# Second layer's input scale from a bound taken when x is written, and late keys turned two ranks later

## The chip, the cores and the metric

One program runs on one core of a Trainium2 chip. The metric is the device time of one execution in microseconds (us), lower is better. The kernel before takes 1208.0 us, the median of three runs (1207.2 to 1209.08).

## The reference

Attention with 32 kept keys per row, followed by two feed-forward layers on the same tokens. Batch 4, 8 heads, 576 tokens, head width 64; the 2304 rows of attention output have 512 columns.

```python
scores = q @ k.T / 8;  kth = 32nd largest of each row
attn = softmax(where(scores >= kth, scores, -1e9))
x = (attn @ v) laid out as (2304, 512)
x = (sigmoid(x @ w_gate) * (x @ w_val)) @ w_out     # 512 -> 1536 -> 512
h = x @ w_in;  out = (relu(h) ** 2) @ w_out2        # 512 -> 2048 -> 512
```

## The kernel before

**Tiles and chunks.** The 2304 rows are 18 tiles of 128. `CHUNKS` groups them: chunks 0 to 5 hold one tile, chunks 6 to 11 hold two (6 and 7, then 8 and 9, up to 16 and 17). A chunk passes through attention, then through both feed-forward layers (`moe32` for chunks 0 and 1 in float32, `moe` for chunks 2 to 11). `attention` runs over units: one head of one tile. Scores of a unit come from four matmuls (`scores`, L395) into S, then VectorE finds the 32 largest in seven rank steps, MAX8 and MATCH_REPLACE8 in turn (`rank`, L406 and L407). ScalarE and GpSimd make the weights, a transposing DMA turns them (PT, L480), and `values16` (L531) multiplies by v and writes x (tile `xs`) for chunks 6 to 11.

**Two float16 halves.** In chunks 2 to 11 each operand of a feed-forward matmul is a pair of float16 tiles, high and low, whose sum stands for the scaled float32 value; a product is three matmuls. So an input needs a power-of-two scale before it can be cut in two. For attention output of chunks 6 to 11 that scale comes from v (`xfac`, `ix`), for chunks 2 to 5 from a sum of squares (`split_x`).

**The second layer's input.** Layer 1 ends in two PSUM tiles, `accs` (L828). `moe` then makes `x2` from them (L854 to L870): ScalarE squares each half (L858), TensorE sums the squares over the partitions with a matrix of ones into `x2pq` (L860, a buffer of the pool `ps_w`), VectorE takes the maximum (L863) and three small steps make the scale `sy` and its inverse `iy` (`pow2_scale`, L140 to L146). Only then ScalarE writes the high half (L867) and VectorE the low half (L868), and the second layer's first matmuls `ph` (L893) can start. In chunks 3 to 10 the program has matmuls of the next chunk's first layer to put in between (`nxt`, `NPRE` = 2 column blocks, `pg` and `pv` at L788); the last chunk, 11, has none.

**Keys.** `prep_keys` loads one head pair's keys of one batch (tiles kn and ke, L161 and L163), transposes them on TensorE into `kpt` (L174), copies the rounded part out on ScalarE (kp, L181), subtracts it on VectorE (L182), and stores both to DRAM (`ks`, four DMAs at L188). Units load them from there (`kst`, L345). Each of the 4 batches has 4 head pairs, so there are 16 such turns. Those of batch 2 are made while chunk 6 is in attention (kpt between 381 and 473 us), those of batch 3 during chunk 8 (600 to 687 us), each at the start of a head pair (`head`), about one chunk ahead of their use.

**Order of the work.** Every engine and every DMA queue runs its instructions in a fixed order. It is made when the program is built: a scheduler that simulates a time line picks, engine by engine, by priorities set around the code (`tc.high_priority`, `at`). All DMAs named here are issued by SyncE (SP), one after another; an issue that waits holds all behind it. The list `later` holds steps put off to a given rank step: `(k, function, arguments)` is run just after rank step k of the unit at hand, and a dependency without a semaphore (`NOSYNC`) tells the scheduler to place the step behind that rank instruction. The kernel uses it for v (`KB`, `KC`). It looked at the first entry of the list alone.

The lines that decide where the second layer may start:

```python
nc.scalar.activation(sq[:, h * KH : (h + 1) * KH], srcs[h], AF.Square)          # L858
nc.tensor.matmul(pq[:, 0:N], ones, sq[:, c], ...)                               # L860
nc.vector.reduce_max(cm, pq[:, 0:N], axis=AX.X)                                 # L863
sy, iy = pow2_scale(cm, small)                                                  # L864
nc.scalar.activation(x2[:, 0, hs], srcs[h], AF.Copy, scale=sy)                  # L867
```

Of the kernel before, what the change touches and what calls it, by code (L numbers as in the profile page):

```python
# [9 lines left out]
BF16 = mybir.dt.bfloat16  # L10
F32 = mybir.dt.float32
F32R = mybir.dt.float32r
I32 = mybir.dt.int32
U32 = mybir.dt.uint32
AF = mybir.ActivationFunctionType
ALU = mybir.AluOpType
# [5 lines left out]
P = 128  # L22
# [48 lines left out]
GLATE = 30.0  # L71
EARLY = ("wg", "wv")
PB = 10
KB = 4
KC = 6
FIRST = 2
# [8 lines left out]
def tile_topk_attention__then__two_moe_layers(  # L85
# [47 lines left out]
    ones = one.to_broadcast([P, P])  # L133


    def pow2_scale(norm, t, squared=True, s=None):

        n = t[:, 0:1]
        shift, e = (24, 62) if squared else (23, 126)
        nc.vector.tensor_scalar(n, norm.bitcast(I32), shift, None, op0=ALU.logical_shift_right)  # L140
        if s is None:
            s = t[:, 1:3]
        nc.vector.tensor_scalar(
            s[:, 0:1], n, -float(2**23), float((127 + e + TB) * 2**23), op0=ALU.mult, op1=ALU.add
        )
        nc.vector.tensor_scalar(  # L146
            s[:, 1:2], n, float(2**23), float((127 - e - TB) * 2**23), op0=ALU.mult, op1=ALU.add
        )
        f = s.bitcast(F32)
        return f[:, 0:1], f[:, 1:2]  # L150
# [5 lines left out]
    def prep_keys(b, hp, keep=False):  # L156

        src = k[b, 2 * hp : 2 * hp + 2]
        kn = apool.tile([P, S], F32, tag="S", bufs=SB, name=f"kn_{b}_{hp}")
        kv = kn[:, 0 : CB * P].rearrange("p (c h d) -> p c h d", c=CB, h=2)  # L160
        nc.sync.dma_start(kv, src[:, 0:SM].rearrange("j (p c) d -> p c j d", c=CB))  # L161
        ke = apool.tile([ST, 2, D], F32, tag="qn", bufs=2, name=f"ke_{b}_{hp}")
        nc.sync.dma_start(ke, src[:, SM:S].rearrange("h p d -> p h d"))  # L163
        kh = apool.tile([P, S], F32R, tag="kst", bufs=KST, name=f"kp_{b}_{hp}")
        kl = kn.bitcast(F32R)
        if keep:
            kl = mpool.tile([P, S], F32R, tag="m4", bufs=M4, name=f"kl_{b}_{hp}")
            kloc[(b, hp)] = (kh, kl)
        for lo, hi in ((0, CB), (CB, NB)):
            pt = ps_t.tile([P, 512], F32, tag="tr", name=f"kpt_{b}_{hp}_{lo}")  # L170
            w = 0
            for c in range(lo, hi):
                kp = P if c < CB else ST
                nc.tensor.transpose(  # L174
                    pt[:, w : w + kp],
                    (kv[:, c] if c < CB else ke).rearrange("p h d -> p (h d)"),
                    ident[0:kp, 0:kp],
                )
                w += kp
            c0 = lo * P  # L180
            nc.scalar.copy(kh[:, c0 : c0 + w], pt[:, 0:w])  # L181
            nc.vector.tensor_tensor(  # L182
                kl[:, c0 : c0 + w], pt[:, 0:w], kh[:, c0 : c0 + w], op=ALU.subtract
            )
        d = dpool.tile([2, 2, D, S], F32R, name=f"ks_{b}_{hp}", tag=f"ks_{b}_{hp}")
        for a, t in enumerate((kh.bitcast(F32), kl.bitcast(F32))):
            for j in range(2):
                nc.sync.dma_start(d.bitcast(F32)[j, a], t[j * D : (j + 1) * D])  # L188
        for j in range(2):
            kscr[(b, 2 * hp + j)] = d[j].rearrange("a d s -> (a d) s")  # L190
# [565 lines left out]
        return xs, ix  # L756


    ahead = {}

    def start(ci):
# [47 lines left out]
    def moe(ci, nxt=None):  # L809
# [42 lines left out]
        KH = KM // 2  # L852
        srcs = [a[:, 0 : KH * N].rearrange("p (d n) -> p d n", d=KH) for a in accs]
        with tc.high_priority(offset=XUP):  # L854
            sq = x2[:, 1].bitcast(BF16)
            pq = ps_w.tile([P, 512], F32, tag="wk", name=f"x2pq_{ci}")
            for h in range(2):
                nc.scalar.activation(sq[:, h * KH : (h + 1) * KH], srcs[h], AF.Square)  # L858
                for c in range(h * KH, (h + 1) * KH):
                    nc.tensor.matmul(pq[:, 0:N], ones, sq[:, c], start=(c == 0), stop=(c == KM - 1))  # L860
            small = mpool.tile([P, 8], I32, tag="sc", bufs=3, name=f"x2s_{ci}")
            cm = small.bitcast(F32)[:, 3:4]
            nc.vector.reduce_max(cm, pq[:, 0:N], axis=AX.X)  # L863
            sy, iy = pow2_scale(cm, small)  # L864
            for h in range(2):
                hs = slice(h * KH, (h + 1) * KH)
                nc.scalar.activation(x2[:, 0, hs], srcs[h], AF.Copy, scale=sy)  # L867
                nc.vector.scalar_tensor_tensor(  # L868
                    x2[:, 1, hs], srcs[h], sy, x2[:, 0, hs], op0=ALU.mult, op1=ALU.subtract
                )  # L870
# [2 lines left out]
                nxt()  # L873
        usc, i2 = layer2_scales()

        us = small.bitcast(F32)[:, 4:6]
        nc.vector.scalar_tensor_tensor(us[:, 0:1], ix, iy, usc, op0=ALU.mult, op1=ALU.mult)
        nc.vector.scalar_tensor_tensor(
# [181 lines left out]
    def attention():  # L1060
# [62 lines left out]
        def tail(n, after=None):  # L1123
# [30 lines left out]
            if j == 1 and i == len(pr.tts) - 1:  # L1154
                if pr.ci < TCI:
                    pr.values()
                    xdone[pr.ci] = pr.hp + 1
                if pr.hp == NHP - 1:
                    if pr.ci in PLAIN:
                        xsp[pr.ci] = pr.xt  # L1160
                    elif pr.ci < TCI:
                        xsp[pr.ci] = split_x(pr.ci, pr.xt)
                    else:
                        xsp[pr.ci] = pr.xt, xfacs[pr.ci][0]

        def orders(n):
            a = [(n - 1, k) for k in range(KA, 7)]
# [29 lines left out]
        for n in range(last + 1):  # L1197
            ci = units[min(n, last - 1)][0].ci
            if ci < TCI:
                with tc.high_priority(offset=int(up[0])):  # L1200
                    head(n + 1)
                    tails((False,))
            if n < last:
                pr, pi, j, i = units[n]
                state[n] = pr.softmax_head(j, i, ready.pop(n))
            for u, k in orders(n):
                if u in state:
                    ins = units[u][0].rank(state[u], k)
                    if k == 0 and prev3 is not None:
                        tc.add_manual_dep(  # L1210
                            ins, prev3.name, NOSYNC, reason="two row blocks at a time"
                        )
                    if k == min(KA, 6):
                        prev3 = ins
                    if k == 6:
                        ends[u] = len(seq)
                    seq.append(ins)
                    while later and later[0][0] == k:
                        _, fn, args = later.pop(0)
                        fn(*args, ins)  # L1220
            turns()
            if ci >= TCI:
                head(n + 1)
                tails((False,))
            tails((True,))
            if n > 0:
                pr, pi, j, i = units[n - 1]
                work[n - 1] = pr.softmax(j, i, state.pop(n - 1))
            turns()
            yield  # L1230
# [166 lines left out]
```

## Time and profile before

| | |
|---|---|
| median of 3 runs | 1208.0 us (1207.2 to 1209.08) |
| profiled execution, its own time | 1210.65 us |
| its span, first to last instruction | 1208.5 us |
| mean granted TensorE clock | 0.987 of 2.4 GHz |
| TensorE matmuls busy | 1154.8 us, 96% |
| VectorE busy | 919.9 us, 76% |
| GpSimd busy | 833.8 us, 69% |
| ScalarE busy | 802.8 us, 66% |

An engine's share is an average over a span with three parts: loading and weight preparation up to about 100 us, attention and feed-forward side by side up to about 1040 us, and feed-forward alone until the end. PE is TensorE's matmuls, DVE VectorE, ACT ScalarE, POOL GpSimd, SP SyncE. A group row of the profile gives busy time, mean duration and the idle time of the engine just before; a row of the timeline gives start, duration, engine, line, what is written and read, the count, and in brackets an idle time before it with what ended it.

### The profile page before, as it was taken

The page shows a single profiled execution, that of the slowest core. Times are in us where ns is not written, and L with a number is a line of the kernel's source. Part 1 is how long each engine was busy: PE and PEld are TensorE (multiplying, and loading weights), DVE is VectorE, ACT ScalarE, POOL GpSimd, SP SyncE. Part 2 cuts the span into 40 slices and gives each one's busy share as a digit, 9 for nine tenths or more (in the row PEclk, how much of TensorE's full clock was granted, in tenths as well). Part 3 has the DMA queues.
Part 4 walks back from the last instruction along what each step waited for, and adds up shares of the span by engine and source line. Part 5 has one row for each costly group of instructions (what it writes and reads, how often), then busy time and mean ns, then how long its engine had stood idle before and what let it go on. Part 6 is the DMA issues. An engine that isn't in the chain of part 4 may idle for free. (4 is left out here: it accounts for less than half of the span.)

```text
span 1208.5 us, 30486 instructions
## 1 busy us (share of the span) xinstructions
PE 1154.8 (96%) x11473; PEld 940.1 (78%) x11473; DVE 919.9 (76%) x1921; ACT 802.8 (66%) x1695; POOL 833.8 (69%) x1294
## 2 busy tenths in 40 slices
PE   7879999999899998999999999999999999999998
PEld 5669878977778877787887688768877886886875
DVE  5999788999998878999998799989899878010010
ACT  5999975877876777777678777676677566222122
POOL 1788964788874786978778877987697669324133
PEclk9889999999999999999999999999999999999999
DMA  8998854324544466656675675665455422100000
GB/s 228 367 347 282 300 153 114 82 86 123 160 118 113 97 147 149 150 128 127 123 173 132 138 157 120 130 149 118 73 106 125 88 49 56 38 1 1 18 1 18
DMA packets 241394, 153.64 MB, mean 127 GB/s; under 512 B 191328, under 2 KB 207712, under 8 KB 241248
## 3 DMA queue, kind: packets, MB, share of 16 engines
q1 hardware_dynamic: 241248, 151.70, 49.5%
q8 instruction: 90, 1.47, 0.5%
q14 instruction: 56, 0.46, 0.1%
HBM read 105.25 MB, written 18.09 MB: 102 GB/s over the span
## 5 line engine op out<-in xcount | busy, mean ns | idle before, releaser
L406 DVE MAX8 mx<-W 128x8 f32<-128x576 f32 x432 | 327.8, 759 | 10.8
L407 DVE MATCH_REPLACE8 W<-mx,W 128x576 f32<-128x576 f32 x288 | 213.9, 743 | 0.0
L893 PE MATMUL ph<-x,wi_w 128*128 128x256 f16 (+1 forms) x1920 | 191.9, 254 | 2.5 <-ACT x L867 1.6
L914 PE MATMUL acc<-w_w,rh 128*128 128x512 f16 x768 | 182.1, 379 | 0.8 <-POOL rh L906 0.8
L893 PEld LDWEIGHTS <-wi_w 128*128 128x128 f16 x1920 | 157.0, 99 | 28.7 <-issue 2.9
L478 POOL TENSOR_TENSOR pp<-S,pp 128x512 f16<-128x512 f32 x192 | 137.1, 736 | 1.7
L395 PE MATMUL sp<-kst,qt 128*128 128x288 f32 x608 | 131.7, 327 | 6.8 <-DMA kst<-ks 4.1
L828 PEld LDWEIGHTS <-wo_w 128*128 128x128 f16 x1440 | 118.0, 98 | 18.0 <-issue 5.0
L788 PEld LDWEIGHTS <-wg_w 128*128 128x128 f16 x1440 | 116.9, 98 | 16.9 <-issue 1.7
L788 PEld LDWEIGHTS <-wv_w 128*128 128x128 f16 x1440 | 117.8, 98 | 15.6 <-issue 3.0
L800 DVE TENSOR_TENSOR th<-pv,th 128x512 f32<-128x512 f32 (+1 forms) x60 | 34.6, 577 | 124.6 <-PE pv L788 118.2
L432 ACT ACTIVATE S<-S,mx 128x576 f32<-128x576 f32 x144 | 111.8, 776 | 26.3 <-DVE mx L406 25.5
L914 PEld LDWEIGHTS <-rh 128*128 128x128 f16 x768 | 72.3, 98 | 72.4 <-POOL rh L906 1.0
L406 DVE MAX8 mx<-S 128x8 f32<-128x576 f32 x144 | 107.2, 745 | 14.6 <-ACT S L398 14.4
L398 ACT COPY S<-sp 128x576 f32<-128x576 f32 x144 | 91.7, 637 | 37.6 <-PE sp L395 33.3
L407 DVE MATCH_REPLACE8 W<-mx,S 128x576 f32<-128x576 f32 x144 | 107.0, 743 | 0.0
L788 PE MATMUL pg<-xs,wg_w 128*128 128x256 f16 x864 | 106.2, 273 | 0.4 <-DVE th L800 0.4
L476 POOL TENSOR_SCALAR S<-S,bs 128x576 f32<-128x576 f32 x96 | 71.9, 749 | 50.0 <-ACT pp L475 43.6
L905 POOL TENSOR_TENSOR r<-r 128x512 f32<-128x512 f32 (+1 forms) x80 | 69.7, 871 | 52.8 <-ACT rh L904 51.5
L788 PE MATMUL pv<-xs,wv_w 128*128 128x256 f16 x864 | 103.7, 273 | 0.5 <-DVE x2s L863 0.5
L828 PE MATMUL acc<-gh,wo_w 128*128 128x256 f16 (+1 forms) x1056 | 102.2, 248 | 1.6 <-POOL gh L804 1.6
L475 ACT ACTIVATE pp<-S,bs 128x576 f16<-128x576 f32 x96 | 74.4, 775 | 42.5 <-issue 21.6
(238 smaller groups left out, 2321.4 us busy)
## 6 DMA issues: line engine op xcount, KB each, us to landing
kst<-ks SPq DMA_DIRECT2D x112, 288.0 KB, 3.2
v<-vd SPq DMA_DIRECT2D x32, 320.0 KB, 3.3
wi_r<-in_moe_w_in_dram SPq DMA_DIRECT2D x16, 512.0 KB, 6.2
w_r<-in_moe_w_out_dram SPq DMA_DIRECT2D x16, 512.0 KB, 4.9
qn<-in_q_dram SPq DMA_DIRECT2D x124, 64.0 KB, 2.6
v<-in_v_dram SPq DMA_DIRECT2D x28, 256.0 KB, 3.1
wg_r<-in_moe_w_gate_dram SPq DMA_DIRECT2D x12, 512.0 KB, 6.1
wv_r<-in_moe_w_val_dram SPq DMA_DIRECT2D x12, 512.0 KB, 7.3
```

What stands on the lines that cost most here:

```text
L395: nc.tensor.matmul(sp[:, e, 0:HALF], l, r, start=(x == 0), stop=(x == len(ops) - 1))
L398: nc.scalar.copy(ss.rearrange("p (e s) -> p e s", e=2), sp[:, :, 0:HALF])
L406: return nc.vector.max(m8, st.cur).ins
L407: ins = nc.vector.match_replace(st.wk, m8, st.cur, NEG).ins
L432: nc.scalar.activation(wk, wk, AF.Prelu, bias=kth, scale=-1.0, alpha=1.0 / BIG)
L475: nc.scalar.activation(pp[:, 0:S], wk, AF.Copy, scale=rz)
L476: nc.gpsimd.tensor_scalar(wk, wk, rz, 1.0, op0=ALU.mult, op1=ALU.mult)
L478: nc.gpsimd.tensor_tensor(pp[:, o : o + e - f], wk[:, f:e], pp[:, f:e], op=ALU.subtract)
L788: nc.tensor.matmul(pp[:, e * N : (e + 1) * N], wblk(wd, a, c, f0, P), xs[:, b_, c, :], start=(e == 0 and n == 0), stop=(n == 3 * KM - 1), ...
L828: nc.tensor.matmul(accs[d // 2][:, (d % 2) * N : (d % 2 + 1) * N], wblk("wo", a, f, d * P, P), gh[:, b_, e * N : (e + 1) * N], start=(f == ...
L893: nc.tensor.matmul(ph[:, e * N : (e + 1) * N], wblk("wi", a, c, f0, P), x2[:, b_, c, :], start=(e == 0 and n == 0), stop=(n == 3 * KM - 1) ...
L914: nc.tensor.matmul(acc2[i][:, 0:DM], gh[:, b_, e * N + i * P : e * N + (i + 1) * P], wblk("w2", a, f, 0, DM), start=(f == 0 and x == 0), s ...
```

## The change

There are three parts. First, `x2` of a chunk no longer waits for its own squares. For chunks 6 to 11 `x_squares` squares the high half of x on ScalarE once x is written (behind rank step `KX` = 1 of a following unit), into the single buffer `vo` that the values' halves use too; `x_norm` sums it with four matmuls into a buffer of `ps_t` (behind rank step `KP` = 5), and makes `sy` and `iy` there, lowered by 2^17 (`X2B`), a bound in which the weights' norms stand. For chunks 2 to 5, whose x was scaled by its own norm already, the scale is the constant 2^-17. Second, the keys of batches 2 and 3 are loaded where they were, but turned behind rank step `KK` = 2 of a following unit (`turn_keys`). Third, the list `later` now runs every entry of the rank step at hand, not the first alone.

```diff
+X2B = 17
+KX = 1
+KP = 5
+KK = 2
+KL = (2, 3)
...
         nc.sync.dma_start(ke, src[:, SM:S].rearrange("h p d -> p h d"))
+        if b in KL:
+            later.append((KK, turn_keys, (b, hp, keep, kn, kv, ke)))
+        else:
+            turn_keys(b, hp, keep, kn, kv, ke, None)
+
+    def turn_keys(b, hp, keep, kn, kv, ke, after):
         kh = apool.tile([P, S], F32R, tag="kst", bufs=KST, name=f"kp_{b}_{hp}")
...
+    def x_squares(ci, xt, after=None):
+        N = len(chunks[ci]) * P
+        sq = apool.tile([P, KM, N], BF16, tag="vo", bufs=1, name=f"xq_{ci}")
+        ins = nc.scalar.activation(sq, xt[:, 0], AF.Square)
+        if after is None:
+            x_norm(ci, sq, N)
+        else:
+            tc.add_manual_dep(ins.ins, after.name, NOSYNC, reason="written by then")
+            later.append((KP, x_norm, (ci, sq, N)))
+
+    def x_norm(ci, sq, N, after=None):
+        pq = ps_t.tile([P, 512], F32, tag="tr", name=f"xn_{ci}")
+        for c in range(KM):
+            mm = nc.tensor.matmul(pq[:, 0:N], ones, sq[:, c], start=(c == 0), stop=(c == KM - 1))
+            if after is not None:
+                tc.add_manual_dep(mm.ins, after.name, NOSYNC, reason="squared by then")
+                after = None
+        t = xsmall[ci]
+        cm = t.bitcast(F32)[:, 3:4]
+        nc.vector.reduce_max(cm, pq[:, 0:N], axis=AX.X)
+        x2s[ci] = pow2_scale(cm, t[:, 5:6], s=t[:, 6:8], lower=X2B)
...
         with tc.high_priority(offset=XUP):
-            sq = x2[:, 1].bitcast(BF16)
-            pq = ps_w.tile([P, 512], F32, tag="wk", name=f"x2pq_{ci}")
-            for h in range(2):
-                nc.scalar.activation(sq[:, h * KH : (h + 1) * KH], srcs[h], AF.Square)
-                for c in range(h * KH, (h + 1) * KH):
-                    nc.tensor.matmul(pq[:, 0:N], ones, sq[:, c], start=(c == 0), stop=(c == KM - 1))
-            small = mpool.tile([P, 8], I32, tag="sc", bufs=3, name=f"x2s_{ci}")
-            cm = small.bitcast(F32)[:, 3:4]
-            nc.vector.reduce_max(cm, pq[:, 0:N], axis=AX.X)
-            sy, iy = pow2_scale(cm, small)
+            sy, iy = x2s.pop(ci, (float(2.0**-X2B), float(2.0**X2B)))
             for h in range(2):
                 hs = slice(h * KH, (h + 1) * KH)
                 nc.scalar.activation(x2[:, 0, hs], srcs[h], AF.Copy, scale=sy)
...
                         xsp[pr.ci] = pr.xt, xfacs[pr.ci][0]
+                        if after is None:
+                            x_squares(pr.ci, pr.xt)
+                        else:
+                            later.append((KX, x_squares, (pr.ci, pr.xt)))
...
-                    while later and later[0][0] == k:
-                        _, fn, args = later.pop(0)
-                        fn(*args, ins)
+                    for x in [x for x in later if x[0] == k]:
+                        later.remove(x)
+                        x[1](*x[2], ins)
```

The lines of the changed kernel stand further down, so L867 is L907 there, L174 is L195, L188 is L212 and L345 is L369.

**ScalarE, last chunk.** The first place is the end of chunk 11's first layer on ScalarE (`gh` is the last block of layer 1, `x_11` is x2 of chunk 11, `r` and `rh` belong to layer 2). Before:

```order
L798 ACTIVATE th_5_17985<-pg_5_17935,ix_15515 128x512
L803 CAST gh_5_17989<-th_5_17985 128x512
L858 ACTIVATE x_11_18064<-acc_11_0_17747 128x512
L858 ACTIVATE x_11_18064<-acc_11_1_17748 128x512
L867 ACTIVATE x_11_18064<-acc_11_0_17747,x2s_18072 128x512
L867 ACTIVATE x_11_18064<-acc_11_1_17748,x2s_18072 128x512
L902 ACTIVATE r_0_18110<-ph_0_18085 128x512
```

Now:

```order
L847 ACTIVATE th_5_17952<-pg_5_17902,ix_15482 128x512
L852 CAST gh_5_17956<-th_5_17952 128x512
L907 ACTIVATE x_11_18031<-acc_11_0_17714,ix_15482 128x512
L907 ACTIVATE x_11_18031<-acc_11_1_17715,ix_15482 128x512
L943 ACTIVATE r_0_18066<-ph_0_18041 128x512
```

The two squares are gone, and the two copies that write x2 follow the last block directly; their scale is in the chunk's `ix` tile, which is written some 40 ScalarE instructions earlier.

**TensorE, a turn of late keys.** The second place is the turn of batch 2's last head pair on TensorE (`sp` are scores, `kpt` the turned keys, `ph` layer 2 of chunk 4, `xp` the product with v). Before:

```order
L788 MATMUL pv_5_1_7107<-xt_5_4951,wv_w1_2432 128x128
L395 MATMUL sp_6_6_7615<-kst_6_6_1_7260,qt_6_3_1_7468 128x288 x3
L174 MATMUL kpt_2_3_0_7586<-ident_81,kn_2_3_7581 128x128 x4
L893 LDWEIGHTS wi_w0_2896
L893 MATMUL ph_4_0_7165<-x2_4_7089,wi_w0_2896 128x128
```

Now:

```order
L555 MATMUL xp_6_2_7571<-PT_6_4_7340,v_6_2_1_6169 64x128
L195 MATMUL kpt_2_3_0_7681<-ident_81,kn_2_3_7548 128x128
L555 LDWEIGHTS v_6_2_1_6169
L555 MATMUL xp_6_2_7571<-PT_6_5_7450,v_6_2_1_6169 64x128
L195 MATMUL kpt_2_3_0_7681<-ident_81,kn_2_3_7548 128x128 x3
L934 LDWEIGHTS wi_w4_3139
```

The transposes stood right behind the scores of head pair 3's first unit (`sp_6_6`) and ahead of `ph_4_0`; now they stand inside a product with v, and `ph_4_0` to `ph_4_3` of layer 2 are ahead of them.

**SyncE, the stores of late keys.** The third place is SP's queue at the first turn of batch 3 (`ks` are the four stores, `kst` the loads of keys for a unit's scores, `PT` the transposing DMAs). Before:

```order
L161 DMA kn_3_0_9708<-in_k_dram 128x8x64
L163 DMA ke_3_0_9710<-in_k_dram 64x2x64
L316 DMA qn_10_1_9729<-in_q_dram 128x2x64
L480 DMA_TRANSPOSE PT_8_7_9601<-pp_8_7_9596 128x9x128
L316 DMA qn_10_1_9729<-in_q_dram 128x2x64
L188 DMA ks_3_0_9724<-kp_3_0_9712 64x576 x2
L188 DMA ks_3_0_9724<-kn_3_0_9708 64x576 x2
L316 DMA qn_11_1_9732<-in_q_dram 128x2x64 x2
L345 DMA kst_8_1_2_9737<-ks_2_0_5421 128x576
L345 DMA kst_8_2_2_9906<-ks_2_1_6197 128x576
```

Now:

```order
L176 DMA kn_3_0_9675<-in_k_dram 128x8x64
L178 DMA ke_3_0_9677<-in_k_dram 64x2x64
L504 DMA_TRANSPOSE PT_8_7_9568<-pp_8_7_9563 128x9x128
L340 DMA qn_10_1_9679<-in_q_dram 128x2x64 x2
L350 DMA v_8_0_2_9325<-vd_2_0_5483 128x1280
L504 DMA_TRANSPOSE PT_9_6_9740<-pp_9_6_9735 128x9x128
L230 DMA ve_3_1_10367<-in_v_dram 64x2x64 x2
L340 DMA qn_11_1_9682<-in_q_dram 128x2x64 x2
L212 DMA ks_3_0_9840<-kp_3_0_9828 64x576 x2
L212 DMA ks_3_0_9840<-kn_3_0_9675 64x576 x2
L369 DMA kst_8_2_2_9873<-ks_2_1_6318 128x576
```

The four stores moved behind the load of v and one transposing DMA, and of the two key loads that stood behind them one (`kst_8_1`) now stands earlier in the queue.

## Rows read from the trace of the kernel before

**Rows 1.** The page's busy times: engine, us busy, share, instructions.

```profile
PE 1154.8 (96%) x11473; PEld 940.1 (78%) x11473; DVE 919.9 (76%) x1921; ACT 802.8 (66%) x1695; POOL 833.8 (69%) x1294
```

**Rows 2.** Windows: stretch, length, busy PE, PEld, DVE, ACT, POOL; clock, DMA share, GB/s.

```profile
480.00:640.00 160.00, 152.78 (x1801) 127.06 (x1798) 147.93 (x319) 116.32 (x262) 124.71 (x221) 1.00 0.64 141
640.00:845.00 205.00, 203.26 (x2012) 159.81 (x2010) 183.48 (x384) 146.77 (x309) 166.48 (x280) 1.00 0.62 134
845.00:1040.00 195.00, 194.79 (x1821) 151.53 (x1820) 158.80 (x327) 127.33 (x256) 144.03 (x225) 1.00 0.42 84
1040.00:1158.40 118.40, 117.88 (x987) 96.33 (x986) 8.99 (x17) 25.90 (x41) 33.57 (x34) 1.00 0.02 5
```

**Rows 3.** Chain of waits, 1148 to 1172 us: start, us, what.

```profile
1150.66 7.88 PE acc L828 x72
...
1158.56 0.61 ACT x L858
...
1160.46 0.70 ACT x L867
...
1161.19 9.69 PE ph L893 x72
```

**Rows 4.** Timeline of TensorE, 1140 to 1165 us.

```profile
1158.36 0.38 PE L860 MATMUL x2pq<-x,ones 128*128 128x256 bf16 x2
```

**Rows 5.** Chain of waits, layers 1 and 2 of chunk 10.

```profile
1039.75 2.62 PE pg L788 x24
...
1080.16 7.86 PE ph L893 x72
```

**Rows 6.** Windows, columns as in rows 2: short stretches with the granted clock.

```profile
472.60:476.10 3.50, 3.31 (x24) 2.93 (x25) 1.96 (x6) 1.34 (x3) 0.31 (x1) 0.51 0.42 104
...
1162.10:1165.60 3.50, 3.50 (x20) 2.49 (x18) 0.49 (x1) 0.00 (x0) 0.00 (x0) 0.51 0.02 5
...
600.00:620.00 20.00, 18.64 (x184) 16.05 (x183) 17.63 (x40) 13.57 (x29) 14.35 (x25) 1.00 0.77 152
```

**Rows 7.** Timeline of TensorE around two turns of batch 2's keys.

```profile
378.25 1.50 PE L788 MATMUL pg<-xt,wg_w 128*128 128x128 f16 x24
...
381.36 0.63 PE L174 MATMUL kpt<-ident,kn 128*128 128x128 f32 x4 [0.88 <-DMA kn<-in_k_dram]
...
468.34 0.64 PE L395 MATMUL sp<-kst,qt 128*128 128x288 f32 x3
472.79 1.12 PE L174 MATMUL kpt<-ident,kn 128*128 128x128 f32 x4 [3.82 <-DMA kn<-in_k_dram]
```

**Rows 8.** Waits of TensorE: who, for what, total us, times, longest us.

```profile
PE kpt L174 <- DMA kn<-in_k_dram: 11.1, 4, 4.4
PE sp L395 <- DMA kst<-ks: 4.1, 6, 0.9
...
PE x2pq L860 <- ACT x L858: 1.4, 4, 0.5
...
PE ph L893 <- DVE x L868: 0.9, 2, 0.6
PE pv L788 <- DVE x2s L863: 0.9, 2, 0.5
```

**Rows 9.** Timelines of SyncE and TensorE, 594 to 612 us.

```profile
600.15 0.60 PE L174 MATMUL kpt<-ident,kn 128*128 128x128 f32 x4
...
605.07 1.18 SPq L188 DMA_DIRECT2D ks<-kn  x2
...
607.48 0.93 SPq L345 DMA_DIRECT2D kst<-ks  x2
...
610.95 0.77 PE L395 MATMUL sp<-kst,qt 128*128 128x288 f32 x4 [0.94 <-DMA kst<-ks]
```

**Rows 10.** The page's costliest groups: busy us, mean ns, idle before.

```profile
L406 DVE MAX8 mx<-W 128x8 f32<-128x576 f32 x432 | 327.8, 759 | 10.8
```

More of the change, by code (lines that the diff above doesn't have):

```diff
@@ L133, in tile_topk_attention__then__two_moe_layers, with pow2_scale @@
     ones = one.to_broadcast([P, P])
-    def pow2_scale(norm, t, squared=True, s=None):
+    def pow2_scale(norm, t, squared=True, s=None, lower=0):
         n = t[:, 0:1]
@@ L143, in pow2_scale @@
         nc.vector.tensor_scalar(
-            s[:, 0:1], n, -float(2**23), float((127 + e + TB) * 2**23), op0=ALU.mult, op1=ALU.add
+            s[:, 0:1],
+            n,
+            -float(2**23),
+            float((127 + e + TB - lower) * 2**23),
+            op0=ALU.mult,
+            op1=ALU.add,
         )
         nc.vector.tensor_scalar(
-            s[:, 1:2], n, float(2**23), float((127 - e - TB) * 2**23), op0=ALU.mult, op1=ALU.add
+            s[:, 1:2],
+            n,
+            float(2**23),
+            float((127 - e - TB + lower) * 2**23),
+            op0=ALU.mult,
+            op1=ALU.add,
         )
@@ L173, in prep_keys @@
                 kp = P if c < CB else ST
-                nc.tensor.transpose(
+                tr = nc.tensor.transpose(
                     pt[:, w : w + kp],
@@ L178, in prep_keys @@
                 )
+                if after is not None:
+                    tc.add_manual_dep(tr.ins, after.name, NOSYNC, reason="loaded by then")
+                    after = None
                 w += kp
@@ L756, in split_x @@
         return xs, ix
+    x2s = {}
+    def x_squares(ci, xt, after=None):
[11 more added lines that the diff above has]
+            mm = nc.tensor.matmul(pq[:, 0:N], ones, sq[:, c], start=(c == 0), stop=(c == KM - 1))
+            if after is not None:
+                tc.add_manual_dep(mm.ins, after.name, NOSYNC, reason="squared by then")
+                after = None
+        t = xsmall[ci]
+        cm = t.bitcast(F32)[:, 3:4]
+        nc.vector.reduce_max(cm, pq[:, 0:N], axis=AX.X)
+        x2s[ci] = pow2_scale(cm, t[:, 5:6], s=t[:, 6:8], lower=X2B)
     ahead = {}
@@ L874, in moe @@
         usc, i2 = layer2_scales()
+        small = mpool.tile([P, 8], I32, tag="sc", bufs=3, name=f"x2s_{ci}")
         us = small.bitcast(F32)[:, 4:6]
```

## The prediction, written before the changed kernel ran

> **What bounds the kernel now.** I read the page's busy times first, then the same by stage, then the chain of waits at the end, then TensorE's own waits, and went to the timeline only where a wait stood. The page says that TensorE is busy 1154.8 us of the 1208.5 us span and VectorE 919.9 us [rows 1]; an average doesn't say who sets the end. The stages do [rows 2]: from 640 to 1040 us TensorE is busy 398 of 400 us, and from 1040 to 1158 us, where attention is over and VectorE works 9 us, 117.9 of 118.4. So from 640 us on the end is TensorE's queue of work, and a gain there needs TensorE to have less to do or to stand still less. From 480 to 640 us it is busy 152.8 of 160 us and VectorE 147.9 of 160; there the two pace each other.
>
> The changed chain shows bare at the end. In chunk 11 nothing of a next chunk is left, and the reader sees one thing after the other [rows 3]: the last 72 matmuls of layer 1, the square of the second half, the copy with the new scale, and only at 1161.19 the first matmul of layer 2. TensorE had no more layer 1 work at 1158.36, where the sum of squares of the first half starts [rows 4].
>
> The late keys show in TensorE's waits. Waiting for kn costs it 11.1 us, 4 times [rows 8]; two of the four are turns of batch 2, the only ones of the four that the change touches: 0.88 us at 381 and 3.82 us at 472.8 [rows 7]. At the second, the scores end at 468.98 and TensorE stands still until the keys land, with all of layer 2 of chunk 4 queued behind the transposes.
>
> **The end of chunk 11.** The second half's square starts at 1158.56 [rows 3], so that half is complete by then, and a copy in its place takes 0.70 us: done at about 1159.26. The first half is complete before it, and layer 2 can start with it at once. The order has eight matmuls on the first half ahead of the first on the second. 24 matmuls of 256 columns take 2.62 us [rows 5], so eight take 0.87 us: from 1158.36 to 1159.23, when the second half is as good as there. The low half of the first part needs one pass of VectorE more and is asked for later still. So layer 2 starts at 1158.36 instead of 1161.19: **minus 2.83 us**. Behind the standstill the clock fell: 0.51 of full from 1162.1 to 1165.6 [rows 6], 1.2 instead of 2.4 GHz, and the first 72 matmuls of layer 2 took 9.69 us [rows 3] where the same 72 of chunk 10, with no standstill ahead, took 7.86 [rows 5]. Without the standstill I expect the full clock: **minus 1.83**. Together **minus 4.7 us**, on the path for certain, as nothing runs beside it.
>
> **The late keys.** Turned behind the third rank step of a later unit, two MAX8 and a MATCH_REPLACE8 at some 0.76 us each [rows 10], they stand 2.3 us later for VectorE, and in TensorE's order several blocks of layer 2 and part of a product with v come ahead of them. So kn has landed, and 3.82 and 0.88 us go: minus 4.7. Right behind the long wait the clock is 0.51 for 3.5 us [rows 6]; half of that time is lost work, 1.7 us, and I let it go with the wait: **minus 6.4** in all. How much of it reaches the end? TensorE is full from 640 us on [rows 2], and VectorE has 12 us of slack from 480 to 640 and 21.5 from 640 to 845 in which attention can follow. I take all of it, and keep zero as the other end: that is attention pacing.
>
> **Matmuls that go.** 4 of the 10 chunks (2 to 5) lose the sum of squares, 16 matmuls of 128 columns; 24 of that size take 1.50 us [rows 7], so 16 take 1.0: **minus 1.0**. The other 24 are moved. Those of chunk 11 leave the standstill for a time when TensorE is full: 4 by 0.109 is **plus 0.4**. The others cost what they cost before.
>
> **Small waits at the other chunks.** TensorE waits 1.4 us for the squares, 0.9 for the low half and 0.9 for a buffer of `ps_w` that `x2pq` holds until the maximum is taken [rows 8]; the longest of the first, 0.5, is in chunk 11's sum already. That leaves 2.7 us at most, 0 at least if another wait takes the place. I take half: **minus 1.3**.
>
> **The new square and its sum.** Six squares of 1024 elements on ScalarE replace pairs of squares of 512 (0.61 us [rows 3]); ScalarE is busy two thirds of the span, and nobody waits for them but the sum. The sum stands in TensorE's order a few matmuls behind a product with v and may wait there for ScalarE. The nearest row is the old sum's wait for its square, at most 0.5 us [rows 8]; six times that is 3.0, none is the other end, and I take one: **plus 0.5**. It now takes a buffer of `ps_t`, which scores' queries and keys use; that is in the same bound. VectorE's four small steps are the same six times and go four times: nothing, since VectorE isn't full.
>
> **SP's queue.** Each turn's four stores now reach SP later and stand ahead of other issues. At 605 us the stores, two key loads behind them and a wait of 0.94 us for these keys follow each other [rows 9]. In the new order one of the two loads is ahead of the stores, so this wait may go (minus 0.9); on the other side each of the eight turns may bring such a wait (plus 7.5). Nearer to the first, as `kst` loads cost TensorE 4.1 us in six waits in the whole span [rows 8]; I take one: **plus 1.0**.
>
> **Sum:** -4.7 - 6.4 - 1.0 + 0.4 - 1.3 + 0.5 + 1.0 = -11.5 us. Against the profiled execution (span 1208.5, 2.15 around it, 1210.65 in all) that gives 1199.15; the median of the runs, 1208.0, lies 2.65 below that execution, so the forecast is **1196.5 us**.
>
> **Rivals.**
>
> *Attention paces.* The keys' gain and the small waits are eaten between 473 and 640 us, where VectorE is busy 92% and TensorE 95% [rows 2]: TensorE then waits for scores or products instead. For it: both are near full there. Against it: VectorE's slack, and TensorE's 398 of 400 us behind it. Left are 4.7 + 1.0 - 0.4 - 0.5 - 1.0 = 3.8 us: **1204.2**.
>
> *The clock falls with the transposes, not with the standstill.* The fall at 472.7 starts where the transposes do. Then it goes where they go, and 1.7 us come back: **1198.2**. Against it: at 600 us the transposes of batch 3 run [rows 9] and the stretch has clock 1.00 [rows 6], while the fall in chunk 11 has no transpose near it. The Trainium skill states this case on the page "TensorE: Matmul & The Clock Gate", part 4, PE-mode transpose: a transpose doesn't count as a busy TensorE in the same way for the clock; by that, the fall would move along with the turns, and the row at 600 us speaks against it here.
>
> *SP's queue turns it round.* The later turns hold the stores, the stores hold key loads and transposing DMAs, and TensorE waits for scores at each of the eight turns as long as the turn is put off, 2.3 us: 18.4 us in place of the 1.0 that I took, **1213.9**, slower than before. It decides from about 1.6 us a turn, (11.5 + 1.0) / 8. For it: key loads land just in time at six places already [rows 8, 9]. Against it: the late keys are used about a chunk later, and the order puts a head's own load ahead of the stores.
>
> **How the numbers follow.** Forecast 0.65, attention paces 0.20, the clock 0.08, SP's queue 0.07. About 0.2%, 2.4 us, is what a measurement here can tell from no change. The forecast, the clock and most of attention's case lie below 1205.6: faster 0.86; part of attention's case and small mishaps of the order: same 0.07; SP's queue: slower 0.07. The low end takes 4.7 + 6.4 + 1.0 + 2.7 + 0.9 - 0.4 = 15.3 us, 1192.7, and lets the redrawn order save 2.7 us of the other waits, since every engine's order is new from about 270 us on: 1190. The high end is attention's case and 0.8 us more for the square's sum: 1205.
>
> **What would show it.** In the profile after: the first `ph` of chunk 11 within 0.3 us of the last `acc` of layer 1, and its 72 matmuls in about 7.9 us at clock 1.00; no wait of `kpt` for kn behind 30 us, and clock 1.00 around 470; `xn` waiting under 0.5 us each time; TensorE's idle time from 140 us on lower by about 8 us. I am wrong on the keys if TensorE's waits for `kst`, PT or `gh` between 380 and 640 us grow by as much as the waits for kn shrink, wrong on the clock if it still falls to 0.5 at the turns or in chunk 11, and wrong on the sign if waits for `kst` rise from 4 to over 16 us.

## The result, and the profile after

The changed kernel takes **1194.5 us**, the median of 4 runs (1193.8 to 1195.76), beside 1208.19 us of the kernel before on the same chip (4 runs, 1207.2 to 1209.08): ratio 0.9885, 95% interval 0.9865 to 0.9904, so 13.9 us less (11.6 to 16.3). The profiled execution took 1193.91 us, its span 1192.1 us. The forecast was 1196.5, with 1190 to 1205 as range.

The page's busy times, as in [rows 1]:

```profile
PE 1155.2 (97%) x11457; PEld 938.2 (79%) x11457; DVE 914.6 (77%) x1905; ACT 799.4 (67%) x1681; POOL 834.0 (70%) x1294
```

TensorE has 16 matmuls less and is busy 0.4 us longer than in [rows 1], in a span 16.4 us shorter. The first half of that is what the change says; the second is a puzzle that the experiments settle.

Windows of the changed kernel, columns as in [rows 2]: stages, then the two places where [rows 6] had clock 0.51.

```profile
380.00:480.00 100.00, 98.19 (x1415) 84.73 (x1413) 87.99 (x203) 75.64 (x188) 78.61 (x147) 1.00 0.58 127
480.00:640.00 160.00, 157.21 (x1800) 131.60 (x1799) 150.22 (x324) 120.23 (x261) 127.82 (x221) 1.00 0.66 149
...
1040.00:1144.00 104.00, 104.00 (x862) 84.05 (x860) 7.04 (x10) 22.39 (x36) 31.79 (x32) 1.00 0.02 6
...
470.00:476.00 6.00, 6.00 (x75) 4.05 (x73) 5.25 (x11) 5.58 (x17) 5.49 (x12) 1.00 0.09 20
1146.50:1150.00 3.50, 3.50 (x34) 3.08 (x32) 1.00 (x2) 0.69 (x1) 0.00 (x0) 1.00 0.00 0
```

From 480 to 640 us TensorE is idle 2.8 us (7.2 in [rows 2]); at 470 and in chunk 11 the clock is whole.

Chain of waits, end of chunk 11, as in [rows 3]:

```profile
1138.69 7.86 PE acc L877 x72
1146.55 7.92 PE ph L934 x72
```

Timeline of ScalarE and TensorE at the same place:

```profile
1145.28 0.69 ACT L907 ACTIVATE x<-acc,ix 128x512 f16<-128x512 f32 x1 [5.14 <-PE acc L877]
...
1146.39 3.83 PE L934 MATMUL ph<-x,wi_w 128*128 128x256 f16 x33
1146.59 0.69 ACT L907 ACTIVATE x<-acc,ix 128x512 f16<-128x512 f32 x1 [0.62 <-PE acc L877]
```

Layer 2 follows layer 1 without a gap: 1138.69 + 7.86 = 1146.55. The copy of the first half ends at 1145.97 (1145.28 + 0.69), 0.4 us before the first `ph` at 1146.39; the second half's runs beside the first matmuls of layer 2. What took 2.83 us in [rows 3, 4] is gone.

TensorE's waits, as in [rows 8]:

```profile
PE kpt L195 <- DMA kn<-in_k_dram: 5.8, 2, 4.3
...
PE xp L555 <- DMA PT<-pp: 2.1, 4, 0.8
...
PE sp L419 <- DMA kst<-ks: 0.6, 1, 0.6
PE acc L877 <- ACT ob L973: 0.6, 1, 0.6
```

Of the four waits for kn the two at the start are left. The waits for x's squares, for the low half and for the maximum [rows 8] are gone, and the new sum `xn` waits for nothing. Waits for `kst` fell from 4.1 to 0.6 us.

Timeline of TensorE at the turn of batch 2's last head pair, where [rows 7] had 3.82 us of standstill:

```profile
469.09 0.77 PE L419 MATMUL sp<-kst,qt 128*128 128x288 f32 x4
469.70 0.40 PE L877 MATMUL acc<-gp,wo_w 128*128 128x128 f16 x4
...
472.05 0.92 PE L555 MATMUL xp<-PT,v 128*64 128x128 f16 x26
472.90 0.33 PE L195 MATMUL kpt<-ident,kn 128*128 128x128 f32 x1
473.16 0.24 PE L555 MATMUL xp<-PT,v 128*64 128x128 f16 x1
473.33 0.55 PE L195 MATMUL kpt<-ident,kn 128*128 128x128 f32 x3
473.71 1.06 PE L934 MATMUL ph<-x,wi_w 128*128 128x128 f16 x16
```

No wait, and no fall of the clock. But the product with v is cut in two by a transpose; that turns out to matter.

**One yardstick for the traces.** The first 230 us have falls of the clock that differ from execution to execution (3.4 to 23.9 us at half clock in the fourteen traces) and have nothing to do with the change. So traces are compared below from the start of the last matmul of chunk 1's first layer (`acc<-g`; at 234.45 us before, at 232.22 us after), up to which TensorE's order is the same in all kernels of the table below: from there to the end it is 974.05 us before and 959.88 after, 14.2 less. Added up over TensorE's instructions in that stretch, idle time fell from 27.4 to 11.5 us, and time at half clock from 6.8 us to none. 15.9 us of idle time and 3.4 us of lost clock are 19.3, more than the 14.2 gained. The rest shows in TensorE's busy time: it should have fallen by 4.4 us (3.4 of clock, 1.0 of the matmuls that went), and rose by 1.7. About 6 us were given back.

### The profile page after: what moved, and what is told of

It reads as the page before. It is cut to its first block, busy times and chain, and to the rows that moved or that the text cites. A ratio compares the mean times of both kernels' runs of the same rounds, so it can differ in the third digit from the quotient of the medians.

```text
span 1192.1 us, 30442 instructions
## 1 busy us (share of the span) xinstructions
PE 1155.2 (97%) x11457; PEld 938.2 (79%) x11457; DVE 914.6 (77%) x1905; ACT 799.4 (67%) x1681; POOL 834.0 (70%) x1294
## 4 chain that ended last, share of the span: by engine, by line
PE 71%; ACT 11%; DVE 6%; POOL 5%; DMA 3%; issue 3%; SPq 1%; ACTq 0%; POOLq 0%
PE ph L934 13%; PE acc L955 13%; PE pv L837 9%; PE pg L837 9%; PE acc L877 9%; PE sp L419 6%; PE xp L555 4%; DVE mx L430 2%; DVE W L431 2%; DMA PT<-pp 2%; PE xp L582 1%; ACT S L472 1%; PE ph L1048 1%; PE qpt L379 1%; PE acc L1065 1%
## 5 line engine op out<-in xcount | busy, mean ns | idle before, releaser
L419 PEld LDWEIGHTS sp<-kst,qt 128*128 128x128 f32 x608 | 89.9, 190 | 11.9 <-POOL qt L395 2.3
```

The source lines that it names most:

```text
L419: nc.tensor.matmul(sp[:, e, 0:HALF], l, r, start=(x == 0), stop=(x == len(ops) - 1))
```

## The experiments

All run beside the kernel before on the same chip. Us against before are the ratio times 1208.2, with its interval. `OLDX` below lists the chunks that keep the old squares, sum and scale (the removed lines of the diff stand behind `if ci in OLDX`).

| run | median, us | against before, us | from the yardstick to the end, us | idle in it, us | pieces of product |
|---|---|---|---|---|---|
| before | 1208.19 | | 974.05 | 27.4 | 70 |
| changed kernel | 1194.5 | -13.9 (-16.3 to -11.6) | 959.88 | 11.5 | 101 |
| chunk 11 only | 1203.39 | -3.0 (-5.2 to -0.8) | 968.22 | 23.4 | 70 |
| late keys only | 1205.04 | -2.1 (-4.3 to +0.2) | 969.42 | 21.9 | 90 |
| late keys of batch 2 only | 1203.3 | -5.2 (-7.2 to -3.0) | 968.11 | 24.9 | 73 |
| new scale only | 1200.34 | -6.3 (-8.5 to -4.0) | 965.04 | 14.5 | 97 |
| new scale only, sum sooner | 1197.87 | -11.2 (-14.3 to -8.1) | 964.46 | 16.8 | 91 |
| before, list alone changed | 1207.45 | one run | 974.48 | 27.0 | 70 |
| changed, sum sooner | 1195.28 | -11.1 (-13.4 to -8.7) | 962.25 | 12.4 | 101 |
| changed, turn behind rank step 0 | 1196.24 | -12.4 (-15.6 to -9.4) | 963.48 | 13.5 | 101 |
| changed, batch 2's turns alone late | 1193.7 | -15.0 (-18.5 to -11.6) | 961.24 | 12.1 | 98 |
| changed, product whole | 1184.47 | -23.6 (-27.1 to -19.9) | 948.31 | 15.4 | 48 |
| before, product whole | 1202.42 | -7.0 (-9.8 to -4.2) | 964.68 | 26.7 | 48 |
| changed, later head first | 1189.3 | -18.0 (-22.0 to -14.1) | 955.37 | 12.4 | 79 |

A piece is an unbroken run of 64-column product matmuls (`xp`, float16) on TensorE, counted in the trace. Six of the traces hold one more fall of the clock behind the yardstick, 3.4 us at half between 315 and 327 us and so 1.7 us of their stretch: the list alone, the new scale only, the changed kernel with the sum sooner, with rank step 0, with batch 2's turns alone late, and with the later head first. It stands behind waits of 1.0 to 1.4 us that the eight others have there too, without a fall.

**The new scale in chunk 11 alone.**

```diff
-KL = (2, 3)
+OLDX = tuple(range(2, 11))
+KL = ()
```

> The kernel before, with the new scale for chunk 11 alone; every engine's order is that of before but for the square, the sum and the copies of that chunk. My step (standstill 2.83 us and clock 1.83 us go, one sum of 0.4 us is added where TensorE is full): 4.3 us faster, 1203.8, no stretch of half clock at the end. Rival, the clock falls at that place whatever TensorE did before: 2.4 us faster, 1205.8, the 72 matmuls of layer 2 still take over 9 us.

Measured 1203.39 us, 3.0 us less than before (0.8 to 5.2). The chain of waits of this kernel at the end of chunk 11, and its windows behind the keys' wait and behind the start of layer 2:

```profile
1147.29 7.86 PE acc L878 x72
1155.15 7.92 PE ph L950 x72
```

```profile
471.00:474.40 3.40, 3.40 (x33) 3.08 (x31) 2.89 (x8) 1.19 (x3) 0.00 (x0) 0.50 0.58 143
1155.00:1159.00 4.00, 4.00 (x39) 3.52 (x37) 1.10 (x2) 0.73 (x2) 0.00 (x0) 1.00 0.02 4
```

The standstill of 2.83 us [rows 3, 4] is gone, and that is the size of what this part gains; the fall at 471 us, behind a wait for kn of 3.52 us, is still there. The interval holds both 4.3 and 2.4 us; what speaks against the rival are the 72 matmuls in 7.92 us at clock 1.00, where it had them over 9.

**The late keys alone.**

```diff
+OLDX = tuple(range(2, 12))
```

> The late turn of the keys of batches 2 and 3 alone, the scale from the squares as before. My step: the waits of kpt for kn at 381 and 473 us (4.7 us) and the half clock behind the second go and reach the end, 6.4 us less and 1.0 us more from SP's queue, 1202.7. Rival, attention paces: the waits go and others of the same size stand between 380 and 640 us, 1207 to 1209. Rival, SP's queue turns it round: waits for kst rise by over 5 us and the kernel is slower than 1208.

Measured 1205.04 us, not surely better than before. The waits for kn behind 30 us and the half clock at 470 are gone, but TensorE's waits from 380 to 480 us are now these:

```profile
PE acc L878 <- ACT ob L989: 1.6, 1, 1.6
PE pv L838 <- DVE x2s L916: 1.3, 2, 0.9
PE xp L556 <- DMA PT<-pp: 1.2, 2, 0.9
PE sp L420 <- ACT S L423: 1.1, 1, 1.1
PE qpt L380 <- ACT xf L570: 1.0, 1, 1.0
PE sp L420 <- ACT qt L392: 0.9, 1, 0.9
```

The windows give 8.2 us of idle time for that stretch (100 - 91.79), and 8.3 before, 4.7 of these for kn. The first wait of the list stood there before too (1.5 us); the others, most of them for work of attention, are new or longer. So with the old squares in place, other waits take over there where the keys' went. In the changed kernel 1.8 us are left.

That isn't the whole account, though. From the yardstick to the end idle time does fall, by 5.5 us, most of it behind 480 us, and 3.4 us of clock come back; the stretch is only 4.6 us shorter. TensorE's busy time took the rest: with the clock taken off it grew by 4.2 us, as the new order has 20 pieces more. What a piece costs is worked out below.

This run also holds the end of chunk 11 as it was, and there its chain differs from before in one thing:

```profile
1144.13 7.87 PE acc L878 x72
...
1153.93 0.70 ACT x L922
...
1154.67 8.02 PE ph L950 x72
```

The same standstill, and the 72 matmuls of layer 2 take 8.02 us, not 9.69 [rows 3]: the clock did not fall.

**The new scale alone.**

```diff
-KL = (2, 3)
+KL = ()
```

> The new scale alone, keys turned where they were. My steps: chunk 11's 4.7 us, 1.0 us of matmuls and 1.3 us of waits less, 0.9 us more: 6.1 us faster, 1202.0, with the wait of kpt for kn of about 4 us and the half clock behind it still there. Rival, the two parts share a gain at 473 us (with x2 of chunk 4 ready sooner TensorE reaches the keys at another time): the wait for kn is much shorter or longer than 3.82 us and the two single gains don't add up to the 13.7 us of both.

Measured 1200.34 us, 6.3 less than before. From 480 to 640 us idle time falls to 2.2 us as in the changed kernel; the wait for kn (3.91 us at 468.87) and half a clock behind it stay. From the yardstick to the end this part is 9.0 us shorter than before, though it has 10.2 us at half clock beside 6.8, and the late keys 4.6; together 13.6, and the changed kernel gained 14.2. The medians of these two add up to 8.4 only, which two further runs (below) look into.

**The sum two rank steps sooner.**

```diff
-KP = 5
+KP = 3
```

> The changed kernel with the sum of squares behind rank step 3 instead of 5: same work, only the order is drawn anew around the six sums. If the 13.7 us rest on the parts and not on one lucky order: within 2 us of 1194.5. If the order itself is worth several us: over 3 us away from it, with TensorE's waits other than those of kpt and x2 changed by as much.

Measured 1195.28 us, ratio 0.9908 (0.9889 to 0.9928). Another order, the same time within 1 us. But it has the same 101 pieces of product, so it can't say what an order is worth; the runs with the product whole, below, put that at 10 us.

**Before, with the list alone changed.** Both parts are undone (`OLDX` all chunks, `KL` empty; these edits aren't shown); only the way in which `later` is run differs.

```diff
-                    while later and later[0][0] == k:
-                        _, fn, args = later.pop(0)
-                        fn(*args, ins)
+                    for x in [x for x in later if x[0] == k]:
+                        later.remove(x)
+                        x[1](*x[2], ins)
```

> The changed source with all three parts set back but the reading of the list: every engine's order is that of the kernel before, so this is a second profile of it. If the half clock follows from the wait for kn and from the standstill in chunk 11, both half stretches (473 us and 1162 us) are there again, 3.4 us each. If it is a matter of where a free-running beat of the clock's regulator stands, one or both are missing with the same waits, and 1.7 us of gain for each belong to no part of the change.

Measured 1207.45 us in one run. The order is that of before, so this is a second look at the same instructions. Windows behind the wait for kn (3.60 us here) and behind the standstill of chunk 11:

```profile
471.50:475.00 3.50, 3.50 (x28) 3.12 (x28) 2.23 (x7) 1.34 (x3) 0.16 (x1) 0.50 0.27 83
1160.00:1163.50 3.50, 3.50 (x35) 3.14 (x33) 1.04 (x2) 0.18 (x1) 0.00 (x0) 1.00 0.02 5
```

The clock fell at the one and not at the other. At the wait for kn it fell before the wait was over, with TensorE still and the transposes (from 471.31) still to come:

```profile
469.90:471.20 1.30, 0.00 (x0) 0.00 (x0) 1.30 (x5) 0.05 (x1) 1.11 (x4) 0.50 0.57 124
```

Over all the traces: of five with the old end of chunk 11 (before, this one, the late keys alone, batch 2's keys alone, before with the product whole) it fell behind that 1.61 us wait in one, the profile of before; of six with a wait for kn of 3.25 to 3.91 us at about 470 us, behind it in all six; of the eight without such a wait, in none.

**The product with v in one piece.** The changed kernel gives about 6 us back, and its TensorE is busy longer with fewer matmuls. Split by form, one group had grown: the product with v. Row of before, then of the changed kernel (columns as in the page's costliest groups):

```profile
L531 PE MATMUL xp<-PT,v 128*64 128x128 f16 x1232 | 47.6, 221 | 2.2 <-DMA PT<-pp 2.1
```

```profile
L555 PE MATMUL xp<-PT,v 128*64 128x128 f16 x1232 | 53.7, 222 | 2.1 <-DMA PT<-pp 2.1
```

Same number, same mean duration, 6.1 us more: they overlap less, and the new order cuts them in more pieces. This is how a cut looks in the changed kernel's timeline, with scores put between the matmuls of one product:

```profile
928.23 0.58 PE L555 MATMUL xp<-PT,v 128*64 128x128 f16 x13
928.73 0.40 PE L419 MATMUL sp<-kst,qt 128*128 128x288 f32 x1
929.06 0.24 PE L555 MATMUL xp<-PT,v 128*64 128x128 f16 x1
929.24 0.40 PE L419 MATMUL sp<-kst,qt 128*128 128x288 f32 x1
...
930.57 0.53 PE L555 MATMUL xp<-PT,v 128*64 128x128 f16 x12
931.03 1.16 PE L877 MATMUL acc<-gp,wo_w 128*128 128x256 f16 x9
```

28 product matmuls and 4 of scores take 2.80 us from 928.23 to 931.03. The 4 scores by themselves take 0.61 (469.09 to 469.70 above). To keep a product whole, it got a priority, and the order of its two heads was turned round, so that the head whose weights land later comes first:

```diff
+XPUP = 5000
...
-                    for j in range(2):
...
+            with tc.high_priority(offset=XPUP):
...
+                        for j in (1, 0):
```

> The changed kernel with the 28 or more matmuls of each product with v kept together (their priority raised, and the head whose transposed weights land later comes first). The order has 48 runs of such matmuls in place of 101 (before the change: 70). Theory: each entry to such a run costs TensorE about 0.14 us that shows as busy, and the redrawn order with its 31 more runs gave back 4.4 us; 53 fewer runs give 7.4 us: 1187, with the matmuls of xp some 7 us shorter from start to next start. Rival, the pieces filled waits and cost nothing: the time stays within 1.5 us of 1194.5 or rises, with xp waiting for PT over 3 us more.

Measured **1184.47 us**, ratio 0.9805 (0.9776 to 0.9835): 10 us below the changed kernel, and better than both kernels. The timeline of this kernel shows a whole product, and the group's row 42.8 us for all of them:

```profile
916.34 0.97 PE L557 MATMUL xp<-PT,v 128*64 128x128 f16 x28
917.24 0.94 PE L839 MATMUL pv<-xs,wv_w 128*128 128x256 f16 x7
```

```profile
L557 PE MATMUL xp<-PT,v 128*64 128x128 f16 x1232 | 42.8, 221 | 4.8 <-DMA PT<-pp 3.9 <-DVE x L910 0.8
```

28 in a row take 0.90 us (916.34 to 917.24). So the cut product above costs 2.80 - 0.90 - 0.61 = 1.29 us for four pieces more, 0.32 us each. Over all pieces, by the starts of neighbouring matmuls and against the usual step of each form, a piece costs 0.09 us where it begins and 0.13 where it ends as a median, 0.23 to 0.25 for both on average; the 0.14 of the theory was too low. 31 pieces more are then 7 to 8 us, and 53 fewer 12 to 13. Here TensorE's busy time from the yardstick on is 15.4 us shorter, its idle time 3.9 longer, the stretch 11.6 shorter. All of the cost counts as busy.

A rival would be that any change from one kind of matmul to another costs as much. The changed kernel's trace tells them apart. In the profile's rows 128\*128 and 128\*64 are the rows and columns of the array that a matmul uses. From the yardstick on, 730 changes between two kinds that both use 128\*128 took 0.00 us more than the usual step as a median (nine in ten at most 0.001), float32 beside float16 too; all 115 changes from 128\*128 to 128\*64 took at least 0.087, and all 107 back at least 0.122.

The Trainium skill has a sentence on it, on the page "TensorEngine Tiling (Array Packing)", Key Properties: "Changing tiling mode (not just tile) drains the TensorE". The traces agree: a price stands at the changes between 128\*128 and 128\*64, and none between two kinds of 128\*128.

**The same on before.**

> The kernel before with the products with v kept together, 48 runs in place of 70. Theory: 22 runs by 0.14 us, 3.1 us faster than before, about 1205; the change's parts then gain more on top of it than 13.7 us. Rival, pieces cost nothing: within 1 us of before.

Measured 1202.42 us, ratio 0.9942 (0.9919 to 0.9965), 7.0 us less than before for 22 pieces fewer. At 0.25 us each these are 5.5, inside the interval; the 3.1 of the theory is below it (4.2 to 9.8). The trace is 9.4 us shorter; 1.7 of that is the clock at the end, which did not fall here, and the rest was not followed further.

**The turn behind rank step 0.** Changed kernel with `KK = 0`.

> The changed kernel with the late keys turned behind rank step 0, two steps (1.5 us) sooner. My step: what counts is that the keys have landed; kn takes 3.3 to 5 us from issue, so some of the turns wait again, up to 1.5 us at one or two of the eight: 1195 to 1197.5. Rival, the order is what matters and not the delay: kpt waits for kn under 0.3 us and the time differs from 1194.5 by the redrawn order alone, up to 3 us either way.

Measured 1196.24 us, ratio 0.9897 (0.9871 to 0.9922), no wait for kn behind 130 us. The waits of up to 1.5 us that were expected didn't come back, so this run shows no cost of a sooner turn, and doesn't show from which point on the turn would wait again.

**Batch 2's turns late, batch 3's early.** Changed kernel with `KL = (2,)`.

> Batch 3's key turns are put as early as before, batch 2's stay delayed. If only a turn that is waited for costs time (the waits of before lay at batch 2's turns), this is within 2 us of the changed kernel, 1192 to 1197 us, and no wait of a turn for the keys' load over 0.5 us stands after 130 us. If the delay itself is what helps, by leaving the turns to later places, batch 3's turns cost something again: 1197 us or more.

Measured 1193.7 us, ratio 0.9876 (0.9847 to 0.9904): as the changed kernel. The waits lay at batch 2's turns; batch 3's delay neither gains nor costs what an interval of 3.5 us to either side could show.

**The later head first, without a priority.**

```diff
-                    for j in range(2):
+                    for j in (1, 0):
```

> The changed kernel with only the order of the two heads in the product with v turned round, and no priority for it; its order has 79 separate runs of such matmuls on TensorE where the changed kernel has 101 and the whole one 48. If what the whole one gained comes from each run's entry and exit, at 0.15 to 0.2 us a run, 22 runs fewer give 3 to 4.5 us: 1190 to 1191.5 us, and the products' busy time falls from 53.7 to about 49.5 us. If it came from the priority (the products being done sooner), this one is within 2 us of the changed kernel.

Measured 1189.3 us, ratio 0.9851 (0.9818 to 0.9883); its group of products:

```profile
L555 PE MATMUL xp<-PT,v 128*64 128x128 f16 x1232 | 48.6, 221 | 2.7 <-DMA PT<-pp 2.7
```

22 pieces fewer, 5.1 us less busy, 4.5 us less from the yardstick on (with 1.7 of clock at 316 us that the changed kernel's trace doesn't have), 5.2 in the medians. The number of pieces decides, not that the products are done sooner.

All the traces say the same. Take TensorE's busy time from the yardstick on, less half of what it was busy at half clock, and with the 1.0 us of the old sums added where they went: that is 930.2 us with 48 pieces and 945.6 with 101 in the changed kernel's orders, and a straight line through all fourteen traces rises by 0.245 us a piece (correlation 0.97).

**Two more orders of the two parts.** Batch 2's turns alone with the old squares (`KL = (2,)`, `OLDX` all chunks), and the new scale alone with `KP = 3`.

> As the run of late keys alone (squares as before), but with batch 2's turns delayed only. Its order has 72 separate runs of product matmuls on TensorE, the kernel before 70, the late keys alone 90. If the late keys' gain was partly given back through the cut products (4.2 us of busy time in the late keys alone), this one keeps it: busy time of the products at about 48 us, and 1199.5 to 1203 us, 4 to 5 us below the late keys alone. If attention paced there and ate the gain, it is at about 1205 us again.

> As the run of the new scale alone (keys as before), with the sum of x's squares two rank steps sooner, so another order of the same part; 90 separate runs of product matmuls, 97 in the new scale alone. If the scale's part is worth about 9 us, as the traces said, 1198 to 1200 us; if it is worth about 6, as that run's median against before said, 1201 to 1203 us. The waits for the keys' load stay at 3 to 4 us at about 470 us, with the clock at half behind.

Measured 1203.3 us (-5.2) and 1197.87 us (-11.2). The first has 17 pieces fewer than the late keys alone. Its busy time is 4.3 us lower, as expected, but its idle time 3.0 higher, so it is 1.3 us shorter in the trace and 1.7 in the medians, not 4 to 5. That fits the rival: with the old squares attention's work paces the stretch from 380 to 480 us (9.1 us of idle time here), and a part of what the cuts cost would otherwise have been idle. The second shows the scale's part at 8 to 14 us where its first order showed 4 to 8.5; the two traces differ by 0.6 us only. Its wait for kn (3.25 us) and the half clock stay, as expected. The single gains add up to 8.4 us in the first pair of orders and to 16.4 in the second, beside 13.9 for both. How the total splits between the parts stays open by several us.

## Why the prediction was right, and where its steps were not

The total came out 2.0 us below the forecast and the sign was right. The mechanisms of the two main terms, the standstill in chunk 11 and the wait for kn, are borne out; that the number is so near is partly luck. Twice as much idle time went as was forecast, and the cut products, which the forecast didn't have, took the surplus back.

- **End of chunk 11, minus 4.7.** The 2.83 us of standstill were right: nothing is left of it in the chain, and chunk 11 alone gives 3.0. The 1.83 us of clock, put down "on the path for certain", were not: the same standstill brought the fall in one trace of five. It was an event of the profiled execution, and 2.65 us had been taken off for that execution already in going to the median.
- **Late keys, minus 6.4.** Both waits and the fall of the clock went, as forecast. Alone the part gives 2 to 5 us: with the old squares other waits come in their place from 380 to 480 us, 8.2 us of idle time as before, and 20 more pieces cost 4.2. The rival that attention paces was right for that stretch, by its mechanism; not in the changed kernel, where 1.8 us of idle time are left there.
- **Matmuls that go, minus 1.0, and plus 0.4 for chunk 11's sum.** The count is right, 11473 to 11457; the time was not measured by itself.
- **Small waits at the other chunks, minus 1.3.** Too small: half of 2.7 was taken, and the whole went, with 1.7 us of waits of `acc` for ScalarE's `ob` (2.3 to 0.6), which were not in the account; they are 0.8 with the new scale alone and 2.8 with the late keys alone, so they go with the scale. The new scale alone gives 6 to 11 us, of which chunk 11 has 3.
- **New square and sum, plus 0.5.** Nothing: `xn` never waits. A square takes 1.06 us, and nothing waits for it.
- **SP's queue, plus 1.0.** Wrong in sign: the waits for `kst` fell from 4.1 to 0.6 us. Part of that is the execution: they are 3.2 to 4.9 us in before, the list alone and chunk 11 only, and 0.6 to 2.3 in the changed kernel and the five runs of it that change `KP`, `KK`, `KL` or the product. The rival with 1213.9 us falls; two rank steps less of delay bring 1.5 us of these waits and no gain.
- **Missing: the redrawn order cuts the products.** "Since every engine's order is new" stood in the low end of the range as a saving of up to 2.7 us; it cost 6 us by the product's busy time, 7 to 8 by the price of a piece, and the pieces could be counted in the order beforehand, 70 against 101.
- **Idle time, about 8 us less.** It fell by 16 from 140 us on. From the yardstick on, waits for kn went by 4.7 us, those for the old squares and for what hung on them by 4.8: 9.5 together, near the forecast's 8. The rest wasn't in it: `kst` 3.5, `ob` 1.7, PT 1.1 (3.2 to 2.1). The last two before:

```profile
PE xp L531 <- DMA PT<-pp: 3.2, 6, 0.8
...
PE acc L828 <- ACT ob L932: 2.3, 2, 1.5
```

- **The clock falls with the transposes.** No: the turns are there, and the clock is 1.00 from 470 to 476 us; the fall goes with the wait for kn, six times of six with it and none in eight without. In three of the six (list alone, new scale only, and that with the sum sooner) it begins inside the wait, 1.1 to 1.5 us before the first transpose. By the page "TensorE: Matmul & The Clock Gate" of the Trainium skill, part 4, PE-mode transpose, a transpose doesn't count as a busy TensorE in the same way; the four transposes at 473 us, 0.9 us among other matmuls, give no sign of it, and what a longer row of them would do is not shown.

The account from the yardstick on: idle -15.9, clock -3.4, fewer matmuls -1.0, and +6.1, by which the product's busy time grew, make -14.2, as measured. By the price of a piece, +7 to +8, it ends 1 to 2 us short.

## What to carry to other kernels

A wait that goes can be replaced by the next one due, unless that goes too: from 380 to 480 us the late keys alone left 8.2 us of idle time, both parts together 1.8. Whether that makes the parts worth more together than apart is not shown, as the sums of the single gains lie on both sides of the whole. Where a scheduler redraws the order, count in the new order how often TensorE changes between matmuls of 64 and of 128 columns, since a busy share hides what each change costs; here keeping the products whole was worth 10 us on top, as much as two thirds of the change. And before a dip of one profiled execution is put in a sum against a median, see whether another trace of the same instructions has it.

## What the runs showed of the hardware

- Going from 128-column matmuls to a run of 64-column ones and back costs TensorE about 0.09 us at the start and 0.13 us at the end as a median (changed kernel), as busy time, 0.245 us a run by the line through fourteen traces; a change between two kinds that both use 128\*128 costs 0.00 (730 of them); inside a run such matmuls follow each other every 0.03 us (28 in 0.90 us).
- Behind a wait of 3.25 to 3.91 us near 470 us the clock was at half for 3.4 to 6.8 us in six traces of six; behind 1.61 us of waiting in chunk 11 in one of five, and the 72 matmuls took 9.69 us there and 8.02 where it did not fall (the late keys alone); behind waits of 1.0 to 1.4 us between 312 and 322 us in six of fourteen.
